# A windowed-attention and feed-forward kernel: who stores tile 0's output blocks, and in what pieces the last values and first weights are cast

## The chip, the cores and the metric

The kernel runs on one core of a Trainium2 chip. The core has five engines with queues of their own: TensorE (PE: matmuls and transposes, with weight loads shown apart as PEld), VectorE (DVE), ScalarE (ACT), GpSimd (POOL) and SyncE (SP, which only issues DMAs). ScalarE and GpSimd issue DMAs too. Engines work side by side and wait for each other through semaphores; each takes its own instructions in the order written.

The metric is the device time of one execution in microseconds (us), the median of several runs.

## What is computed

Attention over 8 batches of 576 positions, 8 heads of 64, in which each position sees only the 32 positions on either side; then a feed-forward layer on the 4608 rows of 512 that result.

```python
scores = scale * np.matmul(q, k.transpose(0, 1, 3, 2))
mask = np.abs(pos[:, None] - pos[None, :]) <= window
scores = np.where(mask, scores, -1000000000.0)
scores = scores - np.max(scores, axis=-1, keepdims=True)
attn = np.exp(scores)
attn = attn / (np.sum(attn, axis=-1, keepdims=True) + 1e-09)
attn_out = np.matmul(attn, v)
...
x = attn_out.transpose(0, 2, 1, 3).reshape(B * S, H * D)
h = x @ w_in
g = 0.5 * h * (1.0 + np.tanh(c * (h + 0.044715 * h * h * h)))
out = g @ w_out
```

Inputs and the output are float32, `w_in` is 512 by 2048, `w_out` 2048 by 512. On the chip everything that TensorE multiplies is 16-bit, so each input is loaded by a DMA and cast.

## The kernel before, in words

The attention of one batch gives 576 rows, transposed into a ring `xT`. The feed-forward layer takes them in nine tiles `t` of 512 rows. All is written into one program in a fixed order (a manual schedule): what stands first in an engine's queue runs first.

**Opening (to about 19 us).** Batch 0's queries and keys are cast, transposed and scored in four groups `g` (two heads each). Values `V` are kept in eight slots: slots 0 to 3 are the four 128-row chunks, cast by `cast_v`; slots 4 to 7 hold the same rows shifted by half a chunk, filled by copies (`pair_chunk`, lines 198 and 200). `times(0, g, o, pe, which)` (line 453) multiplies a group's weights with the named slots. The program runs slots 0, 1 and 4 for all groups, then 2 and 5 group by group, then 3, 6 and 7. Slot 2 is chunk 2 as cast by GpSimd; slot 5 is a copy by VectorE. For the last chunk (3), VectorE casts slot 3 (line 290) and copies its odd half to slot 7 (line 746), and ScalarE casts its even half to slot 6 (line 747). `spread` (line 489, VectorE) scales a group's result into `xT`. `spin` (line 236) is a matmul on zeros whose result nobody reads.

**Tile 0.** `ffn_in` (line 526) multiplies `w_in` with `xT`; `gelu` (line 534, ScalarE) follows. The weights come in four blocks of 512 columns, `wi[0]` to `wi[3]`, each in four chunks of 128 rows, cast by `cast_w` (line 218). Chunk 0 of `wi[0]` is cast by GpSimd, chunk 1 by ScalarE, chunk 2 by GpSimd, chunk 3 by VectorE. The first matmuls go over chunks 0 and 1 for three, then four blocks of 128 columns. Then `ffn_out_0` (line 598) multiplies with `w_out`, whose loads and casts arrive meanwhile; batch 1's attention is woven in between after the table `PLAN_0`. Four output blocks `t4` of 128 rows are evacuated from PSUM in the order 0, 3, 1, 2: blocks 0 and 1 by VectorE into a shared buffer `yo2`, blocks 3 and 2 by ScalarE into `yo` buffers (line 604). They are appended to the list `later` in that order and stored in the next tile.

**Tile 1.** `ffn_in` runs over sixteen columns `fc`, with a GELU behind each. After column 5, `later`'s first (block 0) is stored by ScalarE's queue, and then all but one of the rest, last first (blocks 2 and 1), by GpSimd's; after column 6 the one left (block 3) is stored by ScalarE's. `store` (line 588) issues to GpSimd when no queue is named. Each block of tile 0 is one DMA of 256 KB. After columns 9 to 13, `parts[1]` (the function `rest` in `cast_and_turn`) makes ScalarE cast batch 2's last queries into `qt16` (line 354, four copies) and last keys into `kt16` (line 360), and SyncE issue their transposes (lines 357 and 361). `qt16` has the same buffer (tag `"qt16"`) as `yo2`: its first copy waits until blocks 0 and 1 are stored. Then `ffn_out` (line 624) multiplies out tile 1, with sums and differences of blocks (a scheme of Winograd's kind with seven products), again with the next batch's attention between.

**Later tiles.** The same for `t` = 2 to 8. Queries and keys of the next batch are cast by VectorE (lines 345 and 368) and turned by DMA transposes that SyncE issues (lines 348 and 370); the output rows are stored by GpSimd.

Of the kernel before, what the change touches and what calls it, by code (L numbers as in the profile page):

```python
# [36 lines left out]
def cut(b):  # L37
    return 120 if b else 128
# [33 lines left out]
def kernel(  # L72
# [9 lines left out]
    nc = tc.nc  # L82
# [40 lines left out]
    Vs = [const.tile([128, 8, H, 64], FP16, name=f"V{i}") for i in range(2)]  # L123
    w_in16 = big.tile([128, 4, DF], FP16, name="w_in16")
# [3 lines left out]
    raws = {}  # L128
# [60 lines left out]
    def pair_v(b, copy, hs=slice(0, H)):  # L189

        V = Vs[b % 2]
        copy(V[64:128, 4:8, hs, :], V[64:128, 0:4, hs, :])
        copy(V[0:64, 4:7, hs, :], V[0:64, 1:4, hs, :])
# [22 lines left out]
    def cast_w(w, dst, on_dve=(0, 1), cs=range(4), on_act=()):  # L216
        for c in cs:
            (nc.scalar.copy if c in on_act else nc.vector.tensor_copy if c in on_dve else nc.gpsimd.tensor_copy)(  # L218
                dst[:, c, :], w[:, c, :])
# [13 lines left out]
    def spin(n, width=512, ps=None):  # L233
        ps = psO.tile([128, 512], FP32, name="spin", tag="O") if ps is None else ps
        for _ in range(n):
            nc.tensor.matmul(ps[:, 0:width], idle[:, 0:128], idle[:, 0:width], start=True, stop=True)
# [12 lines left out]
    even, odd = slice(0, 64), slice(64, 128)  # L249
# [39 lines left out]
    def cast_v(b, c, copy=nc.gpsimd.tensor_copy):  # L289
        copy(Vs[b % 2][:, c, :, :], raws[b][3][:, c, :, :])  # L290
# [101 lines left out]
    groups = {}  # L392

    def work_of(b, g):

        if g < 4:
            return (band[:, :, 0:120], [g], MAIN, SLOTS, 0, 120) if b else                 (band[:, :, 0:128], [g], MAIN_0, SLOTS_0, 0, 128)
        p0 = cut(b)
        return (band[:, :, p0:144], range(NPAIR), TAIL if b else TAIL_0, [(7, p0, 144)], p0, 144 - p0)
# [45 lines left out]
    def times(b, g, o, pe, which=range(8)):  # L445
        m, prs, steps, slots, q0, n = work_of(b, g)
        for r, pr in enumerate(prs):
            cols = slice(4 * n * r, 4 * n * r + 4 * n)
            for slot, p0, p1 in slots:
                if slot not in which:  # L450
                    continue
                for h in range(2):
                    nc.tensor.matmul(  # L453
                        o[64 * h:64 * h + 64, cols].rearrange("d (j p) -> d j p", j=4)[:, :, p0 - q0:p1 - q0],
                        Vs[b % 2][:, slot, 2 * pr + h, :],
                        pe[:, h, cols].rearrange("k (j p) -> k j p", j=4)[:, :, p0 - q0:p1 - q0],
                        start=True, stop=True)
# [25 lines left out]
    def spread(b, g, o, lt):  # L483
        n = size(b, g)
        if g < 4:
            pos, done = b * S % RING, 0
            while done < n:
                e = min(n - done, RING - pos)
                nc.vector.tensor_tensor(xT[:, g, pos:pos + e], o[:, done:done + e],
                                        lt[:, done:done + e], op=ALU.mult)  # L490
                done, pos = done + e, (pos + e) % RING
        else:
            pos = (b * S + 4 * cut(b)) % RING
            assert pos + n // NPAIR <= RING
            nc.vector.tensor_tensor(
                xT[:, :, pos:pos + n // NPAIR], o[:, 0:n].rearrange("d (r q) -> d r q", r=NPAIR),
                lt[:, 0:n].rearrange("d (r q) -> d r q", r=NPAIR), op=ALU.mult)
# [9 lines left out]
    def ffn_in(t, n, d0=0, d1=4, then=True):  # L507
        fc = column(t, n)
        if t not in gTs:
            gTs[t] = gp.tile([128, NF, 512], FP16, name="gT", tag="gT")  # L510
        if d0 == 0:
            if t == 0:
                i = n % 8
                if i in (4, 6):
                    phs["S"] = psS.tile([128, 2, 512], FP32, name="ph2", tag=f"S{i // 2 - 2}")
                phs[fc] = psO.tile([128, 512], FP32, name="ph", tag="DO"[i]) if i < 2 else \
                    bank(i - 2) if i < 4 else phs["S"][:, i % 2, :]
            else:
                i = 3 if n in (1, 2) else 0 if n == 0 else (2, 1, 0)[n % 3]
                if n == 1:  # L520
                    phs["S"] = psS.tile([128, 2, 512], FP32, name="ph3", tag="S0")
                phs[fc] = bank(i) if i < 2 else phs["S"][:, n - 1, :] if i == 3 else \
                    psO.tile([128, 512], FP32, name="ph", tag="D")
        ph = phs[fc]
        for dc in range(d0, d1):
            nc.tensor.matmul(ph, w_in16[:, dc, fc * 128:fc * 128 + 128],  # L526
                             xT[:, dc, t * 512 % RING:t * 512 % RING + 512],
                             start=(dc == 0), stop=(dc == 3))
        if d1 == 4 and then:
            gelu(t, n)  # L530

    def gelu(t, n):
        fc = column(t, n)
        nc.scalar.activation(gTs[t][:, fc, :], phs[fc], AF.Gelu_apprx_tanh)  # L534
        if t and n % 4 == 3:
            sums(t, n // 4)
# [20 lines left out]
    def combine(i, eng):  # L557
        dst, x, y = wino["todo"][i]
        eng.tensor_tensor(dst, x, y, op=ALU.subtract)  # L559
# [14 lines left out]
    def store(t, t4, yo, cols=slice(0, 512), *engs):  # L574

        m = i = 0
        while m < 128:
            b, c = divmod(t * 512 + t4 * 128 + m, S)
            q0, n = (0, cut(b)) if c < 4 * cut(b) else (cut(b), 144 - cut(b))
            j, p = divmod(c - 4 * q0, n)  # L580
            e = min(n - p, 128 - m)
            nj = 1 if p else max(1, min(4 - j, (128 - m) // n))
            eng = engs[i % len(engs)] if engs else nc.gpsimd
            if nj > 1:
                e = nj * n
                eng.dma_start(out_v[b, j:j + nj, q0:q0 + n, cols], yo[m:m + e, cols])
            else:
                eng.dma_start(out_v[b, j, q0 + p:q0 + p + e, cols], yo[m:m + e, cols])  # L588
            m += e
            i += 1  # L590

    later = []
# [84 lines left out]
    def pieces(tag, name):  # L677
        return psO.tile([128, 512], FP32, name=name, tag=tag) if tag in "OD" else \
            psS.tile([128, 2, 512], FP32, name=name, tag=tag)[:, 0, :]

    lts, os = {}, {}
# [6 lines left out]
    wi = []  # L688
# [51 lines left out]
    os[3] = pieces("S1", "ps_o")  # L740
    times(0, 3, os[3], groups[(0, 3)], (0, 1, 4))
    spin(3, 512, s0[:, 1, :])
    for g in range(4):
        times(0, g, os[g], groups[(0, g)], (2, 5))
    cast_v(0, 3, nc.vector.tensor_copy)
    nc.vector.tensor_copy(Vs[0][odd, 7, :, :], Vs[0][odd, 3, :, :])
    nc.scalar.copy(Vs[0][even, 6, :, :], raws[0][3][even, 3, :, :])
    for g in range(4):
        times(0, g, os[g], groups.pop((0, g)), (3, 6, 7))
        spread(0, g, os[g], lts[g])  # L750
    for c in range(4):
        cast_w(wi[0], w_in16[:, :, 0:512], (3,), (c,), (1,))
    spin(2, 512, pieces("D", "spin"))
    cast_w(wi[1], w_in16[:, :, 512:1024], (0, 2))
    for dc in range(2):
# [51 lines left out]
    for t in range(NT):  # L807
        b = t + 1
        att = b < B
        if t:  # L810
            for fc in range(begun):
                ffn_in(t, fc, 3, 4, then=False)
            for fc in range(begun):
                gelu(t, fc)
            if att and b > 1:
                parts = cast_and_turn(b)
            for fc in range(begun, NF):
                ffn_in(t, fc)
                if t == 1 and fc == 3:
                    parts[0]()  # L820
                    combine(4, nc.vector)
                if t == 1 and fc in (5, 6):
                    store(0, *later.pop(0), slice(0, 512), nc.scalar)
                if t == 1 and fc == 5:
                    while len(later) > 1:
                        store(0, *later.pop())
                if t == 1 and 6 <= fc < 10:
                    cast_v(2, fc - 6)
                if t == 1 and 9 <= fc < 14:
                    parts[1](fc - 9)  # L830
                if t == 1 and fc == 8:
                    trans_tails(1, psO.tile([128, 8, 128], FP16, name="pt", tag="O"))
                if t > 1 and fc == 8 and att:
                    pair_v(b, nc.vector.tensor_copy)
# [10 lines left out]
        for i in range(113 if t else 65):  # L845
# [3 lines left out]
            for act in plan.get(i, "").split():  # L849
                kind, at = act[0], int(act[act.index("@") + 1:]) if "@" in act else None  # L850
                g = int(act[1:].split("@")[0])
# [101 lines left out]
```

## Time and profile before

| | |
|---|---|
| five runs, us | 305.21, 304.55, 305.84, 305.49, 302.64 |
| median | 305.21 us |
| the profiled execution's own time | 304.27 us |
| its span, first to last instruction | 302.6 us |
| mean granted TensorE clock in it | 0.994 |
| VectorE, ScalarE, GpSimd busy | 64%, 64%, 30% of the span |
| DMA | 50.73 MB, mean 168 GB/s |

The profile is of one execution. Times in its views are us from the span's start; a row has the start, the length, the engine, the line and the operation with the tiles that it writes and reads. Square brackets at the end of a timeline row tell how long the engine was idle before it and what ended that. Matmuls are pipelined: a row of several matmuls ends later than the next one starts, so starts are compared rather than ends. In the chain of waits each piece is what the next one waited for. ACTq, SPq and DVEq are sequencers: instructions that issue DMAs or wait.

The profile's 40 slices show the granted clock in tenths (PEclk) and the busy share of the DMA engines:

```profile
PEclk9979999999999999999999999999999999999999
DMA  7999999999899999898999898989695031004013
```

A slice is 7.6 us long.

### The profile page before, as it was taken

The numbers are of one execution on the slowest core, as the hardware profiler recorded it, in microseconds if no ns is written. First come the engines' busy times: TensorE is split into PE (matmuls) and PEld (weight loads), VectorE is DVE, ScalarE is ACT, GpSimd is POOL, SyncE is SP. The second block draws the span as 40 slices with busy tenths as digits, with TensorE's granted clock in tenths as the row PEclk, the third lists the DMA queues.
The fourth block names the chain that finished last, engine by engine and source line by source line (L and its number), as shares of the span: only waits on it lengthen the run. The fifth ranks groups of instructions, "written<-read, shape, count | busy, mean of one in ns | idle before, by whom it ended". The sixth has DMA issues, their size and how long they took to land.

```text
span 302.6 us, 7119 instructions
## 1 busy us (share of the span) xinstructions
PE 289.7 (96%) x2894; PEld 179.5 (59%) x2894; DVE 194.7 (64%) x436; ACT 193.8 (64%) x307; POOL 90.6 (30%) x140
## 2 busy tenths in 40 slices
PE   7789999999999999998999999999999999999993
PEld 3434443444774588447854785478547864784582
DVE  4654548995966885866687668766875635443452
ACT  4855769469785786577566956685678666606500
POOL 3436435302635050604071426050610050015000
PEclk9979999999999999999999999999999999999999
DMA  7999999999899999898999898989695031004013
GB/s 216 246 357 373 327 287 267 255 258 210 214 168 166 173 245 145 128 112 214 176 179 147 219 181 159 133 211 173 102 180 61 3 94 47 2 9 131 2 42 96
DMA packets 116550, 50.73 MB, mean 168 GB/s; under 512 B 97911, under 2 KB 109943, under 8 KB 116518
## 3 DMA queue, kind: packets, MB, share of 16 engines
q1 hardware_dynamic: 87060, 37.36, 61.8%
q0 software_dynamic: 27776, 10.83, 25.4%
q10 hardware_dynamic: 1682, 2.11, 2.3%
q8 instruction: 22, 0.36, 0.6%
q14 instruction: 10, 0.08, 0.1%
HBM read 36.70 MB, written 9.44 MB: 152 GB/s over the span
## 4 chain that ended last, share of the span: by engine, by line
PE 68%; DMA 21%; SPq 5%; ACT 2%; DVE 2%; issue 1%; POOL 0%; DVEq 0%; ACTq 0%
PE mm L624 32%; PE mm L526 15%; PE ph L526 12%; DMA wst<-in_moe_w_out_dram 6%; DMA KT<-k 6%; DMA wst<-in_moe_w_in_dram 4%; PE ps_s L420 3%; PE ps_d L443 2%; DMA kr<-in_k_dram 2%; SPq L151 2%; DMA out_dram<-yo 2%; PE ps_o L453 2%; DMA tr<-in_k_dram 2%; SPq L209 2%; ACT gT L534 1%; DVE t L559 1%
## 5 line engine op out<-in xcount | busy, mean ns | idle before, releaser
L526 PEld LDWEIGHTS <-w_in 128*128 128x128 f16 x576 | 56.5, 98 | 68.8 <-issue 3.7
L526 PE MATMUL mm<-xT,w_in 128*128 128x512 f16 x304 | 75.8, 382 | 0.5 <-ACT gT L534 0.4
L534 ACT ACTIVATE gT<-mm 128x512 f16<-128x512 f32 x76 | 45.0, 597 | 40.2 <-PE mm L526 39.5
L526 PE MATMUL ph<-xT,w_in 128*128 128x512 f16 x272 | 69.1, 383 | 0.2 <-POOL w_in L218 0.2
L588 POOL DMA_DIRECT2D out_dram<-y x55 | 32.8, 604 | 86.1 <-DVE y L653 76.7
L624 PEld LDWEIGHTS <-s 128*128 128x128 f16 x512 | 49.4, 98 | 6.0
L569 DVE TENSOR_TENSOR s<-gT 128x512 f16<-128x512 f16 x64 | 27.5, 430 | 36.5 <-ACT gT L534 36.5
L534 ACT ACTIVATE gT<-ph 128x512 f16<-128x512 f32 x68 | 37.9, 600 | 15.1 <-PE ph L526 15.1
L624 PE MATMUL mm<-t,s 128*128 128x256 f16 x376 | 45.1, 273 | 0.0
L624 PEld LDWEIGHTS <-gT 128*128 128x128 f16 x384 | 35.7, 98 | 7.2 <-ACT gT L534 0.4
L432 ACT ACTIVATE pe<-ps_s 128x960 f16<-128x960 f32 (+1 forms) x32 | 30.4, 976 | 12.3 <-PE ps_s L420 12.3
L624 PE MATMUL mm<-w_out,gT 128*128 128x256 f16 x256 | 33.3, 273 | 0.1
L97 ACT ACT_TABLE_LOAD x17 | 21.8, 1283 | 2.2 <-issue 1.9
L480 ACT ACTIVATE lt<-lt 128x480 f32<-128x480 f32 (+3 forms) x36 | 21.1, 585 | 1.1
L478 ACT ACTIVATE lt<-ps_d 128x480 f32<-128x480 f32 (+2 forms) x28 | 15.5, 555 | 9.0 <-PE ps_d L443 5.1
L438 DVE TENSOR_TENSOR pe<-pe,band 128x960 f16<-128x960 f16 x28 | 18.4, 680 | 1.2 <-ACT pe L432 1.2
L183 POOL DMA_DIRECT2D V<-in_v_dram x20 | 17.9, 910 | 1.0 <-issue 0.6
L453 PEld LDWEIGHTS <-V 128*64 128x64 f16 x520 | 13.9, 111 | 6.7 <-DVE V L200 3.1
L624 PE MATMUL mm<-t,gT 128*128 128x256 f16 x128 | 16.5, 273 | 0.0
L420 PE MATMUL ps_s<-QT,KT 64*64 64x128 f16 (+3 forms) x576 | 13.8, 216 | 2.1 <-DMA KT<-k 1.9
L847 POOL COPY after<-KL 128x1 f16<-128x1 f16 x5 | 1.7, 338 | 45.8 <-DMA KL<-kt 45.8
L420 PEld LDWEIGHTS <-KT 64*64 64x64 f16 x576 | 10.1, 106 | 8.3 <-issue 4.5
(109 smaller groups left out, 337.1 us busy)
## 6 DMA issues: line engine op xcount, KB each, us to landing
kr<-in_k_dram SPq DMA_DIRECT2D x31, 256.0 KB, 11.2
qr<-in_q_dram SPq DMA_DIRECT2D x6, 1024.0 KB
wst<-in_moe_w_in_dram SPq DMA_DIRECT2D x7, 512.0 KB, 9.4
wst<-in_moe_w_out_dram SPq DMA_DIRECT2D x3, 1024.0 KB, 10.4
V<-in_v_dram POOLq DMA_DIRECT2D x20, 128.0 KB, 8.7
vr<-in_v_dram SPq DMA_DIRECT2D x8, 256.0 KB, 5.7
qr<-in_q_dram SPq DMA_DIRECT2D x7, 256.0 KB, 4.2
out_dram<-y POOLq DMA_DIRECT2D x6, 192.0 KB, 6.3
```

What stands on the lines that cost most here:

```text
L97: nc.scalar.add_instruction(mybir.InstLoadActFuncSet(name=nc.get_next_instruction_name(), act_func_set_id=which, ins=[], outs=[]))
L183: nc.gpsimd.dma_start(V[:, c, :, :], v[b, :, 128 * c:128 * c + 128, :].rearrange("h p d -> p h d"))
L420: nc.tensor.matmul(ps[64 * half:64 * half + 64, h, 4 * n * r:4 * n * r + 4 * n].rearrange("k (j p) -> k j p", j=4)[:, :, p0 - q0:p1 - q0], ...
L432: nc.scalar.activation(pe, ps[:, :, 0:w], AF.Exp, scale=SCALE)
L438: nc.vector.tensor_tensor(pe, pe, m.rearrange("k (o j) p -> k o j p", o=1).broadcast_to(list(pe.shape)), op=ALU.mult)
L453: nc.tensor.matmul(o[64 * h:64 * h + 64, cols].rearrange("d (j p) -> d j p", j=4)[:, :, p0 - q0:p1 - q0], Vs[b % 2][:, slot, 2 * pr + h, : ...
L480: nc.scalar.activation(lt[:, 0:n], lt[:, 0:n], AF.Exp, scale=-1.0)
L526: nc.tensor.matmul(ph, w_in16[:, dc, fc * 128:fc * 128 + 128], xT[:, dc, t * 512 % RING:t * 512 % RING + 512], start=(dc == 0), stop=(dc = ...
L534: nc.scalar.activation(gTs[t][:, fc, :], phs[fc], AF.Gelu_apprx_tanh)
L569: nc.vector.tensor_tensor(dst, x, y, op=op)
L588: eng.dma_start(out_v[b, j, q0 + p:q0 + p + e, cols], yo[m:m + e, cols])
L624: nc.tensor.matmul(pys["apart"][:, 0:256] if apart else py[:, blk, :], lhsT, wino[w][:, f, :], start=(new and i % (8 if one else 16) == 0) ...
```

## The change

Three edits, all in the fixed order of the program.

1. Slot 2 is multiplied for all four groups before slot 5 is, where each group took both in turn.
2. The last values' cast and copies (chunk 3 into slots 3, 6 and 7) are made in two halves of four heads each: VectorE casts, ScalarE casts the even half, VectorE copies the odd half, and again. Chunks 0 and 1 of the first `w_in` block are each cast in two halves of 256 columns, the first by ScalarE and the second by GpSimd; chunks 2 and 3 stay with GpSimd and VectorE.
3. In tile 1, GpSimd's queue stores blocks 0 and 1 (`later[0]` and `later[2]`, those in the shared buffer), and ScalarE's stores block 3 after column 5 (`later[1]`) and block 2 after column 6 (`later[3]`).

```diff
-    for g in range(4):
-        times(0, g, os[g], groups[(0, g)], (2, 5))
-    cast_v(0, 3, nc.vector.tensor_copy)
-    nc.vector.tensor_copy(Vs[0][odd, 7, :, :], Vs[0][odd, 3, :, :])
-    nc.scalar.copy(Vs[0][even, 6, :, :], raws[0][3][even, 3, :, :])
+    for slot in (2, 5):
+        for g in range(4):
+            times(0, g, os[g], groups[(0, g)], (slot,))
+    for hs in (slice(0, 4), slice(4, 8)):
+        nc.vector.tensor_copy(Vs[0][:, 3, hs, :], raws[0][3][:, 3, hs, :])
+        nc.scalar.copy(Vs[0][even, 6, hs, :], raws[0][3][even, 3, hs, :])
+        nc.vector.tensor_copy(Vs[0][odd, 7, hs, :], Vs[0][odd, 3, hs, :])
     for g in range(4):
         times(0, g, os[g], groups.pop((0, g)), (3, 6, 7))
         spread(0, g, os[g], lts[g])
-    for c in range(4):
-        cast_w(wi[0], w_in16[:, :, 0:512], (3,), (c,), (1,))
+    for c in range(2):
+        for i, copy in enumerate((nc.scalar.copy, nc.gpsimd.tensor_copy)):
+            copy(w_in16[:, c, 256 * i:256 * i + 256], wi[0][:, c, 256 * i:256 * i + 256])
+    cast_w(wi[0], w_in16[:, :, 0:512], (3,), (2, 3))
...
                 if t == 1 and fc in (5, 6):
-                    store(0, *later.pop(0), slice(0, 512), nc.scalar)
-                if t == 1 and fc == 5:
-                    while len(later) > 1:
-                        store(0, *later.pop())
+                    for i in (0, 2) if fc == 5 else ():
+                        store(0, *later[i])
+                    store(0, *later[2 * fc - 9], slice(0, 512), nc.scalar)
```

In the built order of instructions this is two more casts or copies on VectorE, two more on ScalarE and one more on GpSimd; the number of matmuls and of DMAs is the same. ScalarE's first copy into `qt16` waits for the two stores on GpSimd's queue, and for the load of the queries as before; before, it waited for one store on ScalarE's queue and one on GpSimd's.

## The prediction

> **What bounds the kernel now.** I read the summary of the page first, then the chain of waits, then the timeline of each engine where the edits lie (15 to 20 us and 57 to 75 us), last the windows and the waits of TensorE downstream.
>
> ```profile
> PE 289.7 (96%) x2894; PEld 179.5 (59%) x2894; DVE 194.7 (64%) x436; ACT 193.8 (64%) x307; POOL 90.6 (30%) x140
> ```
>
> TensorE is the bound: only what takes idle or half-rate time from it counts. In the chain of waits one stretch leaves it:
>
> ```profile
> 62.76 5.34 DMA out_dram<-yo
> ...
> 68.20 0.62 ACT qt L354
> ...
> 72.81 0.50 ACT gT L534
> 73.30 0.05 issue
> 73.35 0.50 PE mm L624 x3
> ```
>
> A store of tile 0 (issue 62.76) holds back ScalarE's first copy into `qt16`, and the copies and GELUs behind it then run back to back until 73.30, when TensorE gets what it waits for. ScalarE's and TensorE's timelines show the same place:
>
> ```profile
> 66.38 0.60 ACT L534 ACTIVATE gT<-ph 128x512 f16<-128x512 f32 x1 [0.42 <-PE ph L526]
> 68.20 0.62 ACT L354 CAST qt<-qt 16x512 f16<-16x512 f32 x1 [1.23 <-DMA out_dram<-yo]
> ```
>
> ```profile
> 67.90 1.03 PE L526 MATMUL ph<-xT,w_in 128*128 128x512 f16 x4
> 69.36 2.02 PE L526 MATMUL mm<-xT,w_in 128*128 128x512 f16 x8 [0.43 <-ACT gT L534]
> 71.35 1.02 PE L526 MATMUL ph<-xT,w_in 128*128 128x512 f16 x4
> 72.35 1.50 PE L624 MATMUL mm<-w_out,gT 128*128 128x256 f16 x10
> ```
>
> The other place is the end of batch 0's attention. TensorE waits for values, and the columns of the windows (length, busy time and count of PE, PEld, DVE, ACT, POOL, then granted clock) show what follows:
>
> ```profile
> 17.54 0.32 PE L453 MATMUL mm<-pe,V 128*64 128x64 f16 x8 [1.12 <-DVE V L200]
> ...
> 19.38 0.95 PE L526 MATMUL ph<-xT,w_in 128*128 128x512 f16 x2 [0.15 <-POOL w_in L218]
> ```
>
> ```profile
> 16.10:19.50 3.40, 2.07 (x45) 1.09 (x44) 2.17 (x6) 2.25 (x5) 1.23 (x2) 1.00 1.02 319
> 19.50:22.90 3.40, 3.40 (x9) 1.18 (x8) 2.47 (x6) 1.10 (x1) 1.65 (x3) 0.50 1.05 405
> 22.90:26.30 3.40, 3.40 (x17) 1.51 (x16) 1.09 (x3) 2.06 (x4) 1.99 (x3) 1.00 1.05 386
> ```
>
> Right after the patchy window TensorE runs 3.4 us at a clock of 0.50: 9 matmuls where the next window has 17.
>
> **Part 1, the stores.** `qt16` takes the buffer of `yo2`, which holds blocks 0 and 1 of tile 0. Before, GpSimd stores blocks 2 and 1 (issues at 58.16 and 59.31) and ScalarE stores 0 and 3, behind the GELUs of its own queue (62.76 and 63.62). After, GpSimd stores 0 and 1 and ScalarE 3 and 2. Same four DMAs, same bytes, same two on each queue; no matmul moves. Block 0 is evacuated by VectorE at 56.59 + 0.68 = 57.27, block 1 at 58.32 + 0.68 = 59.00. GpSimd is idle there, its issues take 0.74 and 0.55, and its stores of these blocks took 4.6 us to land (median, table of DMA issues). So they land at about 57.3 + 4.6 = 61.9 and 59.3 + 4.6 = 63.9. The load that the copies read (issue 58.67) made its last semaphore update at 64.30. The copies stand behind the GELU of 66.38, which ends at 66.98; so nothing but that GELU holds them, with 2.7 us to spare. What is late next: ScalarE's stretch from 68.20 to 73.30 is the same 5.10 us of work started at 66.97 (the 1.23 us of idle time gone), so it ends at 72.07. TensorE for its part: 16 matmuls from 67.90 at 0.216 (1.73 us for 8, from 66.17 to 67.90) end at 71.36, and the eighth of the next line, which needs the last-but-one GELU, comes 7 x 0.109 later ((1.91 - 0.27) / 15 from the row of 16 at 75.22): 72.12. It starts at 73.35 now. Gain 73.35 - 72.12 = 1.23 us. Bounds: 0 if the stores or the load land after 68.2, 1.23 if before 66.98. I take 1.23, since both rows of the same queue lie 3 us inside. The blocks left to ScalarE land near 68 as they do now; their buffers have no later user, and of SyncE's later loads those that take turns with them on a semaphore start at 69.86 and after.
>
> A rule speaks against this part. The Trainium skill, "SBUF — State Buffer", section "SBUF: two separate sides", warns that a GpSimd DMA's descriptors starve while VectorE runs some copies, and gives 620 ns alone against about 3100 ns. The rows here disagree: 0.74 and 0.55 while VectorE was busy without a gap from 56.59 to 62.69. By that page each issue would last 3.1 us, the second would land near 68, and about nothing would be gained.
>
> **Part 2, values and first weights.** The third values' cast by GpSimd (16.25 + 0.61 = 16.86) releases slot 2, which now comes first for all four groups, eight matmuls from 16.92; slot 5 still waits for VectorE's copy (17.48). TensorE's idle time is cut in two, not shortened at the end. The last values: VectorE needs 0.41 for the cast and 0.29 for the copy, ScalarE 0.62. In halves VectorE has two more instructions and ScalarE one. Half a cast on VectorE lies between half of 0.41 and all of it, half a copy likewise; the four together take 0.70 to 1.40. I take 0.95 (0.27 and 0.21 each, nearer to halves: ScalarE's logarithm of 256 columns takes 0.40 against 0.59 for 512). So the first half is ready at about 17.9 instead of 18.15, the second at 18.36. TensorE finishes group 0 at 18.03 instead of 18.25, and VectorE starts the first `spread` at 18.36 instead of 18.53: `xT` is ready at 19.0 instead of 19.17. If each instruction cost its full price, VectorE would be free at 18.8 and this would lose 0.3. The first weight chunk lands near 18.68; 0.61 on GpSimd ends at 19.32. Halves on ScalarE (0.40) and GpSimd (0.31 to 0.61, taken 0.35) end at 19.08. The second chunk, until now ScalarE's alone by 19.30, ends by 19.5, and its first reader comes three matmuls after the first. So the first matmul starts at 19.11 instead of 19.38: 0.27 gained, bounds -0.1 and 0.3. GpSimd's third chunk waits for its DMA until 20.02 either way, and ScalarE's table load is covered until the GELU at 24.09.
>
> The half-rate window is the larger stake. Summed over the trace's matmuls, columns streamed at 0.216 us per 512 fill 0.46 of 12.7 to 16.1, which was followed by full clock, and 0.36 of 16.1 to 19.5, which was not. Starting dense matmuls 0.27 earlier lifts the second to 0.44: between the two, so either answer is open. A window at half rate costs 3.41 / 2 = 1.71 us of TensorE. Not all of it is to be had: the `w_out` cast for fc 4 ends at 40.29, set by its DMA, and its matmul starts at 41.21, so at most 0.92 reaches later stages. Part 2 is therefore worth 0.27 to 0.92; I take the middle, 0.60. The Trainium skill, "TensorE: Matmul & The Clock Gate", section "What's actually happening", calls the window 3413 ns long and free-running; the rows agree on the length, and one run can't show the second, by which the answer would change from run to run.
>
> **Sum.** 0.60 + 1.23 = 1.83 us. The profiled execution took 304.27 (span 302.6 and 1.67 around it), so 302.44 on its terms. It lies 0.94 below the median of five, 305.21; on that basis 305.21 - 1.83 = 303.38, the forecast: 303.4, between 302.4 (full clock) and 304.4 (only two thirds of the stores' gain).
>
> **Rivals.**
>
> *It adds up to more.* One of the five runs took 302.64 without any change, 2.57 under the median, so the kernel has waits that can vanish together. The largest that I see is this one, for key transposes:
>
> ```profile
> 137.07 0.62 PE L420 MATMUL ps_s<-QT,KT 64*64 64x96 f16 x32 [1.64 <-DMA KT<-k]
> ```
>
> If an earlier start (SyncE's loads follow ScalarE's last small copies from 74.76 on) dissolves that wait, and the half-rate window too, the low run becomes the rule: 302.64 - 1.83 = 300.8. Against it: the query transposes ahead of the wait (issue 123.44) follow VectorE's work at the start of that stage, which moves with TensorE.
>
> *Given back.* The same wait speaks for this: if the transposes' landing near 137 is set by traffic (the DMA row of the page is at 8 to 9 tenths until 200 us) and not by their issue, TensorE arrives earlier and waits longer. All gain up to there is gone: 305.2, or 304.6 if a third stays. The same time comes out if the stores don't release `qt16` in time.
>
> *Slower.* The transposes take longer. In tile 2's stage the queries' transpose was issued at 93.00 and landed at 102.1, 9.1 us; in tile 3's it took 12.7 us. The first keys behind it landed at 102.9 in tile 2's stage, 2.1 us before TensorE came at 105.02. Shifted against loads and stores, the transposes could take 12.7 there also: 3.6 - 2.1 = 1.5 us lost in that stage, and as much in the next three, 305.21 - 1.83 + 4 x 1.5 = 309.4; with one stage only, 304.9. It decides where the queries' transpose takes over 11.2 us (9.1 + 2.1). Against it: the bytes and their order on SyncE's queue stay the same.
>
> **How the numbers follow.** Forecast 0.44, more 0.27, given back 0.20, slower 0.09. Leaving out the lower half of "more" and most of "slower" gives 300.8 to 305.3. About 1% is what a measurement of this kernel can tell from no change; faster by over that means under 302.16: nearly all of "more" and the lowest end of the forecast, 0.30. Slower by it, over 308.26: two thirds of the slow rival, 0.06. The rest, 0.64, lies within.
>
> **What would show it.** The stores: ScalarE's first `qt` copy within 0.1 us of the GELU before it, no wait of TensorE between 67 and 73 us, the stretch from the matmuls of 67.90 to the one of 73.35 shorter by 1.2. Still naming a store in front of that copy would prove part 1 wrong. Part 2: matmuls on slot 2 near 16.9 and the first `w_in` matmul about 0.27 earlier; a clock of 1.00 or 0.50 in the window after it tells which price applied. The key wait near 137: under 1 us for "more", over 3 for "given back"; waits for keys near 104 for "slower".

## The result and the profile after

| | before | after |
|---|---|---|
| median of all runs, us (number) | 304.85 (71) | 304.40 (36) |
| lowest and highest, us | 302.57, 310.28 | 301.78, 307.31 |
| the profiled execution's own time, us | 304.27 | 305.94 |
| its span, us | 302.6 | 304.2 |
| its mean granted clock | 0.994 | 0.993 |
| VectorE, ScalarE, GpSimd busy | 64%, 64%, 30% | 64%, 64%, 30% |

The ratio is 0.9973, with a 95% interval of 0.9955 to 0.9991: 0.82 us less, between 0.27 and 1.37. That is inside the predicted range and within 1%, and on the side that was forecast, but less than half of the 1.83 us of the sum. The profiled execution of the changed kernel is one of its longer ones, so its span says nothing of the verdict; it is read here for what happens in it. Medians are of all runs; ratios leave out a kernel's slow executions, so that the two can differ a little.

The first place of the prediction is ScalarE's first copy into `qt16`. ScalarE's timeline after, at the GELU that stands ahead of that copy:

```profile
68.16 0.60 ACT L534 ACTIVATE gT<-ph 128x512 f16<-128x512 f32 x1 [0.44 <-PE ph L526]
68.65 0.60 ACT L354 CAST qt<-qt 16x512 f16<-16x512 f32 x1
69.16 0.58 ACT L534 ACTIVATE gT<-mm 128x512 f16<-128x512 f32 x1
```

The copy has no bracket: it starts 0.49 us after the GELU, the same pitch as the next instruction behind it. GpSimd's timeline after has the two stores that now release it:

```profile
59.36 0.74 POOL L588 DMA_DIRECT2D out_dram<-yo  x1 [1.32 <-DVE yo L604]
61.09 0.81 POOL L588 DMA_DIRECT2D out_dram<-yo  x1 [1.00 <-DVE yo L604]
```

They landed at 64.31 and 66.62 by their last semaphore updates, 2.0 us before the copy. TensorE's timeline after, from there to the end of the woven attention:

```profile
69.69 1.03 PE L526 MATMUL ph<-xT,w_in 128*128 128x512 f16 x4
70.55 1.89 PE L526 MATMUL mm<-xT,w_in 128*128 128x512 f16 x8
72.28 1.03 PE L526 MATMUL ph<-xT,w_in 128*128 128x512 f16 x4
73.14 1.25 PE L624 MATMUL mm<-w_out,gT 128*128 128x256 f16 x10
...
79.15 0.21 PE L453 MATMUL ps_od<-pe,V 128*64 128x96 f16 x2
81.31 0.38 PE L453 MATMUL ps_od<-pe,V 128*64 128x64 f16 x12 [1.96 <-DVE V L193]
```

The wait of 0.43 that stood in the second row before is gone. From the row of 69.69 (67.90 before) to the eighth matmul of the output product (73.14 + 7 x 0.109 = 73.90; 73.35 before) it is 4.21 us instead of 5.45: 1.24 less, against 1.23 predicted. But the last row shows a wait that before did not have: 1.96 us for the values of batch 2. The chain of waits after leads to it:

```profile
60.00 7.07 DMA kr<-in_k_dram
...
67.19 1.43 DVE k L368 x4
...
72.09 0.14 SPq L370
...
72.29 0.57 SPq L376
...
73.53 1.60 SPq L376
...
75.18 4.53 DMA qr<-in_v_dram
...
79.76 0.62 POOL V L290
...
80.84 0.43 DVE V L193
...
81.31 0.38 PE ps_od L453 x12
```

Read from the bottom: TensorE waits for VectorE's copy of the values, that for GpSimd's cast, that for SyncE's loads of the values, and these stand in SyncE's queue behind the key transposes (line 370), which wait for VectorE's key casts and for the keys' load. ScalarE's copies are nowhere in it.

The second place is the opening. TensorE's timeline after, at the first matmuls on slot 2, on the last values, on the first and second pair of `w_in` chunks and on `w_out`:

```profile
17.07 0.25 PE L453 MATMUL mm<-pe,V 128*64 128x64 f16 x4
...
17.98 0.37 PE L453 MATMUL mm<-pe,V 128*64 128x64 f16 x12 [0.47 <-ACT V L748]
...
19.25 0.59 PE L526 MATMUL ph<-xT,w_in 128*128 128x512 f16 x2
...
22.69 0.60 PE L526 MATMUL ph<-xT,w_in 128*128 128x512 f16 x2 [1.55 <-POOL w_in L218]
...
37.78 0.61 PE L598 MATMUL mm<-w_out,gT 128*128 128x512 f16 x2 [1.94 <-DVE w_out L218]
```

Slot 2's matmuls start at 17.07, and the idle time at the values is 0.47 instead of 1.12. The first `w_in` matmul comes 0.13 earlier (19.25 for 19.38). Then TensorE waits for loads: 1.55 for the next `w_in` cast and 1.94 for the first `w_out` cast, neither of which it did in before's profile. The windows after show the granted clock (last but two) with TensorE's busy time (second number):

```profile
16.10:19.50 3.40, 2.87 (x55) 1.55 (x52) 2.65 (x8) 3.35 (x8) 1.04 (x3) 1.00 0.91 257
19.50:22.90 3.40, 1.85 (x9) 0.66 (x8) 1.78 (x4) 0.65 (x1) 0.87 (x1) 1.00 1.04 367
...
78.20:81.60 3.40, 1.44 (x25) 0.89 (x25) 1.19 (x4) 0.94 (x1) 1.70 (x3) 1.00 0.43 85
81.60:85.00 3.40, 3.40 (x35) 2.40 (x30) 3.23 (x8) 2.82 (x5) 2.30 (x4) 0.50 0.94 264
85.00:88.40 3.40, 3.40 (x68) 2.55 (x67) 1.08 (x2) 2.19 (x3) 2.02 (x3) 1.00 1.50 247
```

The window from 19.5 is at full clock now, and yet has nine matmuls, as before: what the clock gave was lost to the wait of 1.55. (Runs 2 and 3 below, with the same opening, do not have that wait.) And the half-rate window has not gone from the profile. It comes at 81.6, right behind the new wait.

### The profile page after: what moved, and what is told of

Read it like the earlier page. It is cut to its first block, busy times and chain, and to the rows that moved or that the text cites. A ratio compares the mean times of both kernels' runs of the same rounds, so it can differ in the third digit from the quotient of the medians.

```text
span 304.2 us, 7124 instructions
## 1 busy us (share of the span) xinstructions
PE 289.9 (95%) x2894; PEld 180.1 (59%) x2894; DVE 193.9 (64%) x438; ACT 194.0 (64%) x309; POOL 90.8 (30%) x141
## 4 chain that ended last, share of the span: by engine, by line
PE 74%; DMA 14%; SPq 6%; DVE 2%; POOL 1%; issue 1%; ACT 0%; DVEq 0%
PE mm L624 31%; PE mm L526 19%; PE ph L526 16%; DMA wst<-in_moe_w_out_dram 6%; DMA kr<-in_k_dram 4%; DMA wst<-in_moe_w_in_dram 3%; PE ps_s L420 3%; SPq L151 2%; PE ps_d L443 2%; SPq L175 2%; PE ps_o L453 2%; DMA qr<-in_v_dram 1%; SPq L376 1%; PE ps_od L443 1%; DVE s L569 1%; PE py L624 1%
## 5 line engine op out<-in xcount | busy, mean ns | idle before, releaser
L526 PE MATMUL mm<-xT,w_in 128*128 128x512 f16 x304 | 74.7, 379 | 0.2 <-DVE yo L604 0.2
L526 PE MATMUL ph<-xT,w_in 128*128 128x512 f16 x272 | 68.2, 379 | 1.6 <-POOL w_in L218 1.6
L588 POOL DMA_DIRECT2D out_dram<-y x55 | 33.1, 610 | 88.4 <-DVE y L653 78.2
L624 PE MATMUL mm<-w_out,gT 128*128 128x256 f16 x256 | 34.0, 278 | 0.0
L624 PE MATMUL mm<-w_out,s 128*128 128x256 f16 x120 | 14.4, 273 | 0.0
L569 DVE TENSOR_TENSOR s<-s,gT 128x512 f16<-128x512 f16 x32 | 13.6, 425 | 1.1
```

The lines of the kernel that those rows point to most:

```text
L569: nc.vector.tensor_tensor(dst, x, y, op=op)
L624: nc.tensor.matmul(pys["apart"][:, 0:256] if apart else py[:, blk, :], lhsT, wino[w][:, f, :], start=(new and i % (8 if one else 16) == 0) ...
```

## The experiments

Two accounts were set against each other. In one, what is won at the `qt` copies reaches the end of the kernel, and more delay there costs as much. In the other the wait for batch 2's values takes it back, and only the opening, the clock or chance is left to explain a difference. Medians below are those of the runs of the kernel before on the same chip; "not resolved" means that the interval of the ratio holds 1. All diffs are against the kernel named.

**1. The stores alone.** Before, with the third edit of the change and none of the other two.

> Only the change of the stores, the opening as before. Theory 1 (the stall is gone and TensorE's gain reaches the end): no wait of TensorE between 67 and 74 us, 1.23 us less than before, so 303.6 against the 304.85 of before. Theory 2 (the gain is met by a later wait for batch 2's values or keys, which come with the loads and not with TensorE): the stall is gone all the same, but a wait for values near 80 us or for keys near 104 or 137 us takes its place, and the time is within 0.4 us of before.

304.37 against 305.86; ratio 0.9976 (0.9939 to 1.0013), not resolved. No idle time before the `qt` copy. TensorE's timeline has the new wait:

```profile
78.85 0.38 PE L453 MATMUL ps_od<-pe,V 128*64 128x64 f16 x12 [1.75 <-DVE V L193]
```

So the wait for the values comes with the store edit, not with the opening.

**2. The opening alone.** Before, with the first two edits.

> Only the opening's changes (slot order, halves), the stores as before. Theory 1: first w_in matmul 0.2 to 0.4 us earlier against the landing of the third values, 0.3 to 0.9 us less in all, 304.2. Theory 2 (weights arrive by DMA and TensorE only waits for them a little later): first matmul earlier, but a wait for w_in or w_out chunks of the same length follows, time within 0.2 us of before.

304.47 against 305.86; 0.9986 (0.9951 to 1.0022), not resolved. The stores hold the first `qt` copy for 3.90 us here, much more than before's 1.23. TensorE's timeline:

```profile
71.05 2.02 PE L526 MATMUL mm<-xT,w_in 128*128 128x512 f16 x8 [3.09 <-ACT gT L534]
...
80.70 0.38 PE L453 MATMUL ps_od<-pe,V 128*64 128x64 f16 x12 [0.20 <-DVE V L193]
```

With 3.09 us lost at 71.05, the wait for the values is only 0.20: where the one wait is long, the other is nearly gone.

**3. The changed kernel again,** for a second profile of it.

> The changed kernel once more, for a second profile of it. If the wait of 2.0 us for batch 2's values near 81 us in the first profile belongs to the change, it stands here too, above 1 us; if it comes from how fast the loads were in that one execution, it is under 0.5 us. Time 0.8 us below before by the measured ratio.

304.31 against 305.86; 0.9959 (0.9922 to 0.9996). No stall before the `qt` copy; TensorE's timeline shows the `w_out` wait and the value wait again, with sizes of their own:

```profile
34.94 0.61 PE L598 MATMUL mm<-w_out,gT 128*128 128x512 f16 x2 [0.97 <-DVE w_out L218]
...
79.58 0.45 PE L453 MATMUL ps_od<-pe,V 128*64 128x64 f16 x12 [2.06 <-DVE V L193]
```

**4. Block 0 stored later still.** Before, with blocks 0 and 3 stored by ScalarE's queue after columns 7 and 8 instead of 5 and 6; blocks 2 and 1 go by GpSimd's, as before:

```diff
-                if t == 1 and fc in (5, 6):
-                    store(0, *later.pop(0), slice(0, 512), nc.scalar)
-                if t == 1 and fc == 5:
-                    while len(later) > 1:
-                        store(0, *later.pop())
+                if t == 1 and fc == 5:
+                    for i in (3, 2):
+                        store(0, *later[i])
+                if t == 1 and fc in (7, 8):
+                    store(0, *later[2 * fc - 14 - (fc == 8)], slice(0, 512), nc.scalar)
```

> The kernel before with ScalarE's two stores issued two columns later (after 7 and 8) and blocks 2 and 1 on GpSimd as before. The store of block 0 then lands about 2 x 0.865 us + 0.4 later and holds ScalarE's first copy for 3 us and more. Theory 1 (what is lost or won at that place reaches the end one to one): about 2 us slower, 306.9. Theory 2 (loads set the next wait): under 1 us slower, 305.6, with less waiting downstream.

303.68 against 305.86; 0.9973 (0.9938 to 1.0007), not resolved, and if anything faster. ScalarE's timeline shows the stall that was meant:

```profile
68.41 0.62 ACT L354 CAST qt<-qt 16x512 f16<-16x512 f32 x1 [2.76 <-DMA out_dram<-yo]
```

It costs TensorE 1.96 us at 69.57, and there is no wait for the values behind it. This is the run against the first account, which had asked for 2 us more (a ratio near 1.007): a longer stall at the very place that the change cleared costs nothing that can be measured.

**5 and 6. The values loaded first.** If the value loads are all that is late, they should go ahead of the transposes in SyncE's queue. After (5) and before (6), with batch 2's four value loads moved:

```diff
-            if b == 2:
-                vr = rawp.tile([128, 4, H, 64], FP32, name="qr")
...
-                raws[b] = [None, None, None, vr]
+        if b == 2:
+            vr = rawp.tile([128, 4, H, 64], FP32, name="qr")
...
+            raws[b] = [None, None, None, vr]
         queries(qr, q16, 0, 128)
```

> The changed kernel, with the four loads of batch 2's values issued by SyncE ahead of that batch's query and key transposes instead of behind them (the transposes are needed at about 104 us, the values at about 79). Theory 2 (the gain of the stores is met by the wait for these values): the wait of 1.9 to 2.2 us near 80 us is gone, and the time is about 2 us below the changed kernel, 302.3 by the medians. Rival (the DMA engines are full, and whatever is moved ahead delays something else as much): the wait is gone or shorter, but one for w_out, queries or keys replaces it, and the time is within 0.5 us of the changed kernel.

> The kernel before with the same move of the four loads. Theory 2: the store's stall of ScalarE near 68 us stays and is now what counts, so the time is that of before or at most 0.5 us less, and it lies 1.2 us or more above the changed kernel with the same move. If the stall grows because the loads now run ahead of ScalarE's stores, TensorE's wait near 70 us is over 1.5 us.

306.44 and 306.51 against 305.02; 1.0034 (1.0000 to 1.0069) and 1.0032 (0.9999 to 1.0066). TensorE's timeline of the first of the two (run 5):

```profile
74.98 0.62 PE L420 MATMUL ps_s<-QT,KT 64*64 64x96 f16 x16 [2.82 <-DMA KT<-k]
```

The wait for the values is gone and the keys are late instead. I had taken batch 2's keys to be needed near 104 us; they are read in tile 1, from 74 us on. In run 6, on the old stores, TensorE loses 1.69 at 70.69 to the stall and then 2.05 at 77.24 to the keys. Values and keys stand in the same queue, and neither order is free.

**7. The opening delayed.** After, with four more matmuls on zeros ahead of the first `w_in` matmul: `spin(2, ...)` becomes `spin(6, ...)`.

> The changed kernel with four more matmuls on zeros ahead of the first w_in matmul, which delays TensorE by 4 x 0.216 = 0.86 us there. If TensorE's place in the opening counts (as my 0.60 us for part 2 has it), it is 0.86 us slower than the changed kernel. If the w_in and w_out loads set the pace there, the wait in front of the first w_out matmul (1.1 and 1.9 us in the two profiles of the changed kernel) is shorter by up to 0.86 and the time is within 0.4 us of the changed kernel.

305.79 against 305.02; 1.0010 (0.9972 to 1.0048), not resolved. The first `w_in` matmul comes at 20.03 instead of 19.25. TensorE's timeline around the first `w_out` matmuls, the only wait there:

```profile
36.02 0.39 PE L598 MATMUL py<-w_out,gT 128*128 128x512 f16 x1 [0.47 <-DVE KT L319]
```

No wait for `w_out`, and tile 1 starts at 56.28, earlier than in both profiles of the changed kernel (59.11 and 57.27). In this profile the 0.8 us of delay have not reached tile 1. That the `w_out` wait swallowed them is not shown: the first profile of before has the same wait of 0.47 and none for `w_out` either, with no delay added, and tile 1's start differs by 1.84 between the two profiles of the changed kernel. The time speaks the other way: its ratio to before is 1.0010 where the changed kernel's is 0.9973, 1.1 us more, near the 0.86 of the first account, though the intervals overlap. The profile, with a value wait of 3.58 us at 80.11, does not say why. So this run leaves open whether TensorE's place in the opening counts.

**8 and 9. Fewer loads.** After (8), and before with the stores of run 4 (9), with one of batch 2's four value loads left and cast four times, so that three quarters of those values are not read and batch 2's output rows are not those of the reference:

```diff
-                for c in range(4):
+                for c in range(1):
...
-                    cast_v(2, fc - 6)
+                    nc.gpsimd.tensor_copy(Vs[0][:, fc - 6, :, :], raws[2][3][:, 0, :, :])
```

> The changed kernel with one of the four loads of batch 2's values, cast four times: three loads of 256 KB are left out, and the output rows of batch 2 are not the reference's. If the late values are what meets the stores' gain, the wait near 80 us is gone and the time is 1.5 to 2 us below the changed kernel, 302.5. If another load takes over at once, less than 0.5 us.

> The kernel with the late stores (e4) with the same three loads left out. With the loads out of the way the stall of ScalarE must cost what it is long: 2 us or more above e8, which is where e4 and the changed kernel were alike. If it costs nothing here either, TensorE's place at this point doesn't count for another reason.

302.74 and 303.62 against 304.81; 0.9945 (0.9916 to 0.9974) and 0.9969 (0.9938 to 1.0000). I had expected the wait for the values to go in run 8. TensorE's timeline says otherwise:

```profile
79.64 0.38 PE L453 MATMUL ps_od<-pe,V 128*64 128x64 f16 x12 [1.90 <-DVE V L193]
```

The first load stands behind the key transposes whether three more follow it or none. So leaving out three quarters of the bytes does not shorten the wait; the place in the queue is what run 8 left as it was. The two kernels don't isolate what they were made for. In run 9 the stall (2.51 before the copy, 1.71 of TensorE at 69.50) is there and no value wait: its tile 1 takes 35.15 us, that of run 8 34.81. Run 9 was expected 2 us or more above run 8; by the medians it is 0.88, and the intervals overlap. Run 8 is 1.7 us below before by its ratio. Part of that goes with the clock: its mean granted clock is 0.9977 over twelve runs, that of before on the same chip 0.9944 over 29, and 0.0033 of 304 is 1.0 us (an estimate).

**10. The values between the key transposes.** After, with the value loads behind the first key transpose instead of both: the block of lines is put into the loop of `keys()`, under `if b == 2 and pr == 1`.

> The changed kernel with the four value loads of batch 2 issued between the two key transposes of that batch. The first keys keep their place (needed at about 72 us), the second are needed at about 77. If order on SyncE's queue is all, the wait for values is under 0.5 us, none for keys comes, and the time is 1.5 us below the changed kernel, 303. If the DMA engines set the pace, a wait for the second keys near 77 to 81 us of 1 us or more takes its place.

Medians 304.94 against 304.81; 0.9971 (0.9937 to 1.0006), not resolved. The means of all executions are 304.71 and 304.70, so nothing is seen to be gained. TensorE's timeline:

```profile
77.70 0.62 PE L420 MATMUL ps_s<-QT,KT 64*64 64x96 f16 x16 [2.41 <-DMA KT<-k]
```

The value wait is gone, and the second key transpose is late by about as much.

**11. The values by GpSimd.** After, with batch 2's values loaded and cast in one step by GpSimd's queue, right behind its two stores, and the casts left out:

```diff
-                if t == 1 and 6 <= fc < 10:
-                    cast_v(2, fc - 6)
+                if t == 1 and fc == 5:
+                    load_v(2)
```

> The changed kernel with batch 2's values loaded by GpSimd's queue (cast on the way, as the later batches' are) right behind its two stores, some 10 us earlier than SyncE gets to them, and GpSimd's four casts gone. If order on SyncE's queue is all, no wait for values or keys between 67 and 85 us and about 2 us below the changed kernel, 302.3. If the DMA engines set the pace, the keys' transposes land later and TensorE waits for them at about 73 us, 1 us or more.

308.71 in six runs against 304.81 (five of the six between 307.24 and 309.86, one at 301.44; no interval). TensorE's timeline, in which the scores have line 416:

```profile
78.67 0.61 PE L416 MATMUL ps_s<-QT,KT 64*64 64x96 f16 x16 [6.77 <-DMA KT<-k]
```

SyncE's queue is relieved of the four loads, and yet this wait for keys is the longest of all runs. SyncE's issue of the two key transposes takes 8.09 us here (from 66.78), against 4.26 in the changed kernel (from 67.98).

**12. The kernel before again,** for a second profile of it.

> The kernel before, for a second profile of it. In every profile so far in which a store held ScalarE's first copy (before, e2, e4), TensorE's wait for batch 2's values near 80 us was under 0.4 us, and in every one without (after, e1, e3, e7) it was 1.8 us or more. If the one takes the other's place, this profile has a stall of ScalarE of 1 us or more before its first copy, and a wait for values under 0.5 us. If the short wait in the first profile was luck with the loads, both waits stand here together. Ratio to before 1.000 within its interval.

305.30 against 305.08; 1.0015 (0.9982 to 1.0049). The stall is 2.41 before the `qt` copy, twice that of the first profile. TensorE's timeline:

```profile
72.52 2.02 PE L526 MATMUL mm<-xT,w_in 128*128 128x512 f16 x8 [1.61 <-ACT gT L534]
...
82.18 0.38 PE L453 MATMUL ps_od<-pe,V 128*64 128x64 f16 x12 [0.20 <-DVE V L193]
```

In the waits of TensorE here there is no `KT` wait near 137, so the 1.64 that before's first profile had there is not a fixture of that kernel. No version with its output whole is resolved as faster than the changed kernel: the lowest ratios to before are run 3's 0.9959, which is that kernel, and 0.9971 to 0.9976 in runs 10, 4 and 1.

**Seven profiles side by side,** those of the runs that neither move or leave out loads nor add matmuls. Worked out from the timelines, in us. The stall is ScalarE's idle time before its first `qt` copy. "To the first output product", "last value cast ends" and "all of tile 1" count from tile 1's first `w_in` matmul, the last of them to tile 2's first matmul. The last column tells where tile 1 has a stretch with a granted clock of 0.50, from the windows.

| kernel | stall | tile 1 starts | to the first output product | last value cast ends | TensorE's wait for values | all of tile 1 | half rate |
|---|---|---|---|---|---|---|---|
| before | 1.23 | 57.32 | 15.03 | 19.39 | none | 33.28 | none |
| before again (12) | 2.41 | 59.31 | 16.21 | 21.44 | 0.20 | 34.73 | none |
| opening alone (2) | 3.90 | 56.35 | 17.69 | 22.92 | 0.20 | 36.25 | none |
| stored later (4) | 2.76 | 56.01 | 17.55 | 20.99 | none | 35.62 | 71.0 to 74.4 |
| after | none | 59.11 | 14.03 | 21.26 | 1.96 | 35.43 | 81.6 to 85.0 |
| after again (3) | none | 57.27 | 14.03 | 21.36 | 2.06 | 35.52 | 79.7 to 83.1 |
| stores alone (1) | none | 56.85 | 14.03 | 21.06 | 1.75 | 33.89 | none |

The stores' edit brings the first output product to 14.03 in every case, 1.0 to 3.7 us sooner than with the old order. The last value cast ends at about the same place with the stall and without (means 21.19 and 21.23), and TensorE waits more than 0.2 us for it only where there is no stall. (Run 7, the changed kernel with matmuls added, fits: 14.03, then 22.89 and a wait of 3.58.) At the end of tile 1 nothing of the gain is to be seen: 34.97 us as the mean of the four kernels with the stall, 34.95 as that of the three without. The wait for values does not make all of that. The column up to the first output product and the wait for values, added up, come to 16.72 on average with the stall (run 4's half-rate stretch among it) and 15.95 without, so up to 0.77 would be left. What remains of tile 1 takes 18.1 to 18.4 us in five profiles and 19.4 in the two with a half-rate stretch there (after and run 3). So the wait gives back most of what the stores win, and the clock behind it more, when it drops. With 3 us between single profiles, no mean here is firm to better than a microsecond.

## Why the prediction was right in its number, and where not

**The stores.** Each step of part 1 up to the output product held, within 0.01 us of the 1.23: the order, the landing ahead of the GELU (2.0 us of room for 2.7 argued), the copies back to back, the matmul that comes 1.24 sooner. The weighing of the page held too. The Trainium skill, "SBUF — State Buffer", section "SBUF: two separate sides", gives about 3100 ns instead of 620 for a GpSimd DMA that overlaps a VectorE copy which locks GpSimd out. The rows after have 0.74 and 0.81 for GpSimd's two issues, with VectorE adding weights and casting queries meanwhile. So that cost did not come; whether VectorE's work there is of the kind that the page means, no run here shows.

**The step that failed is "What is late next".** It followed ScalarE's stretch and stopped at TensorE's first output product; the sum then carried the 1.23 us to the end in full. What is late next is TensorE's read of batch 2's values, 5.45 us further on (79.35 less 73.90). In the changed kernel's profile TensorE comes to it at 79.35 (81.31 less 1.96), and VectorE's two copies take 0.86, from 80.41 to 81.27. So the last cast would have to end near 78.45, 19.3 us after tile 1's start; it ended at 80.37. Before's first profile has these rows in its timelines of GpSimd, VectorE and TensorE:

```profile
76.10 0.61 POOL L290 CAST V<-qr 128x512 f16<-128x512 f32 x1 [0.68 <-DMA qr<-in_v_dram]
...
77.81 0.42 DVE L192 COPY V<-V 64x1024 f16<-64x1024 f16 x1
78.24 0.42 DVE L193 COPY V<-V 64x768 f16<-64x768 f16 x1
...
78.60 0.49 PE L453 MATMUL ps_od<-pe,V 128*64 128x96 f16 x14
```

The last cast ends at 76.71, and VectorE, busy with other work until then, takes up its copies at 77.81. The values were early by 1.10 us, less than the 1.23 that were to be gained. That was to be seen before the change. By that one profile the gain would still have nearly fitted, but it was the luckiest: the other six have the last cast 1.6 to 3.5 us later (20.99 to 22.92). In the other three with the stall the copies begin 0.52, 0.52 and 1.64 us after the last cast (runs 12, 2 and 4), against stalls of 2.41, 3.90 and 2.76: there too the values were early by less than the stall. In those without the stall a wait of about 2 us stands in its place.

**The rival "Given back"** was right in kind and wrong in place. It looked for the return at the key transposes near 137; there TensorE does not wait in the changed kernel's first profile, 0.38 in its second, and not at all in before's second. "Slower" did not come, and "It adds up to more" neither: the key wait near 137 did go, as that rival asked, but it goes without the change as well.

**The opening.** The durations were about right, and no gain from them is shown. VectorE's half cast took 0.28 and its half copy 0.23 (0.27 and 0.21 predicted); ScalarE's two half casts of weights took 0.71 together where 0.40 each was taken, GpSimd's two 0.80 where 0.35 each. The first `w_in` matmul stands at 19.24 as the mean of the three profiles with the new opening (19.25, 19.10, 19.38). With the old one it stands at 19.38, 20.81, 19.12 and 19.00; the mean is 19.58, but 19.17 without the 20.81 of run 12, whose clock was 0.50 from 15.7 to 19.1. So the 0.27 does not show. At tile 1's start the means are 57.37 (57.32, 59.31, 56.85, 56.01) and 57.58 (59.11, 57.27, 56.35): nothing is left, with 3 us between single profiles. The lower bound of 0.27, meant as sure to last, has nothing to rest on. A candidate for what sets the pace there is the loads of `w_out`: the waits before the first `w_out` matmul are 1.94, 0.97 and 0.37 with the new opening (after, runs 3 and 2) and none, 2.17, 1.20 and 0.64 with the old one (before, runs 12, 1 and 4). Run 7, made to test it, did not decide it.

**The clock.** The larger stake, the window from 19.5, went as the sum had hoped in the changed kernel's first profile. But such a stretch in the opening is a matter of the single execution: it stands in before (19.5), in run 12 (15.7), and with the new opening in run 2 (15.2) and run 3 (14.9, the changed kernel itself), and in no other of the fourteen profiles. That is two of six with the old opening and two of eight with the new. The mean granted clock is 0.9932 over the 110 runs of before taken beside the experiments and 0.9932 over the 36 of after. One half-rate window takes 3.41 / 2 / 304 = 0.0056 of it; by that measure 6 of the 36 runs of after have no such window (mean 302.5 us), 20 have one (304.2) and 10 have two (305.3). These counts are estimates, because the clock is also halved at the very end, behind the last matmul (run 1: 0.51 from 297.9 to 300.6, full before, 0.996 as the mean). Nothing shows that the change made such windows fewer.

**What stays open** is which part makes the measured 0.8 us. The stores alone and the opening alone were not resolved from the kernel before, run 4 with its late stores has a ratio like the change itself (0.9973), and the profiles show tile 1 equally long either way. On the chip of runs 1 to 4 all four kernels, run 4 among them, have medians 1.4 to 2.2 us below that of before, so the difference there does not sort by either part. From tile 2 on the rest takes 209.7 to 210.3 us in six of the seven profiles, and 211.9 in before's first, which has the `KT` wait of 1.64. So the number came out inside the range by less gain in both parts, not by the sum as it was put, and in part by luck: the range of 300.8 to 305.3 is wide enough to hold the 305.21 that it started from.

## What to carry to other kernels

When a stall is taken out, follow the bottleneck engine past the stall to the next thing that it reads from outside, and ask by how much that thing was early: if it was early by no more than the stall, the stall was its cover. A wait that is absent because another comes first has no idle time to show; its margin can still be read, from the end of the last step that feeds it to the start of its use (here 76.71 to 77.81). One profile gives one draw of the loads' timing: here the last cast ranged over 3.5 us between seven profiles, more than the gain that was being summed.

## What was not expected of the hardware

The same program has half-rate windows in different number and place from run to run: the changed kernel's first profile has one before its end (81.6), its second has two (14.9 and 79.7). By the means above each goes with some 1.4 us (an estimate). The Trainium skill, "TensorE: Matmul & The Clock Gate", section "What's actually happening", calls the window free-running; one profile could not show that, and the spread over 36 runs of one kernel agrees with it.

A wait of about 2 us for the values is often followed by a half-rate window: after 78.2 to 81.6, with 1.44 us of TensorE busy, the clock was 0.50; in run 3, after 1.34 us busy from 76.3 to 79.7, 0.50 too. In run 1 the same stretch, with 1.65 busy, was followed by full clock, and in run 8, with a wait of 1.90, the clock stayed full too. So the wait can cost its length and more, 1.0 to 1.3 us by the rest of tile 1 in the seven profiles, or not.

In run 11, batch 2's four value loads, moved from SyncE's queue to GpSimd's and started earlier, went with a wait of 6.77 us of TensorE for the key transposes of SyncE's queue, which had less to do than before. Whether the DMA engines that the two queues share do it, or the earlier start, was not tried.
